# Cos-MLP on float16 pairs, with scales from sums of squares and weight units read and split in two stages

## The chip, the cores and the metric

The kernel runs on one core of a Trainium2 chip. The metric is the device time of one execution in microseconds (us); lower is better. Engines are called by their short names: PE (TensorE), DVE (VectorE), ACT (ScalarE), POOL (GpSimd), SP (the queue that issues the DMAs).

## The reference, cut to what matters

```python
attn = softmax(scale * q @ k.T + decay, causal) @ v      # 4 batches, 8 heads, 576 tokens, 64 wide
x = attn as [2304 tokens, 512]
h = x @ w_in                                             # w_in  [512, 2048] float64
g = h * cos(h)
x = g @ w_out                                            # w_out [2048, 512] float64
P = sinkhorn(softmax(x @ w_gate))                        # 8 experts
out = sum over e of P[:, e] * (relu(x @ w1[e]) @ w2[e])  # w1 [512, 1024], w2 [1024, 512]
```

The two weights of the Cos-MLP come in as 64-bit numbers, and the kernel turns them into 32-bit ones by bit operations.

## The kernel before

There are three stages, one after the other: attention (0 to about 237 us of the span), the Cos-MLP (to 654 us) and the experts (to the end).

**Attention** walks through 16 pairs of heads, seven steps each (112 steps, counted by `x`). In each step the code issues work for PE, then ACT, DVE and POOL, and calls `next(pieces)` every third step (lines 727 to 738). When a pair is done, PE turns its output (`turn_x`, L638), ACT copies it from PSUM to `xf` (`keep_x`, L641) and POOL splits it into a rounded part and a rest (`split_x`, L645 and L646), which go to `XT`.

**The Cos-MLP** holds every operand as a pair: `hi`, the number rounded to the PE type fp32r, and `lo`, the rest. A product is three matmuls (`PASSES`: hi·hi, hi·lo, lo·hi). Tokens are cut into five chunks `CH` of 384, 384, 512, 512 and 512; the 2048 hidden columns into 16 units of 128, in blocks of 3, 4, 5 and 4 units (`BLOCKS`). The 80 items of the main loop are (block, chunk, unit). For item n the code issues `layer1(n)` (12 matmuls, L170), then `layer2(n - 2)` (12 matmuls into four PSUM banks, L831), then `between(n)`:

```python
        nc.scalar.activation(t.bitcast(I32), h, AF.Identity, bias=quarter, scale=INV)      # L187
        nc.vector.scalar_tensor_tensor(t, h, INV, t.bitcast(I32), ALU.mult, ALU.subtract)  # L189
        nc.scalar.activation(t, t, AF.Sin, scale=TWO_PI, bias=shift)                       # L190
        nc.vector.tensor_tensor(h, h, t, ALU.mult)                                         # L193
        nc.scalar.copy(hi, h)                                                              # L194
        nc.vector.tensor_tensor(lo, h, f32(hi), ALU.subtract)                              # L196
```

Inside `between` the code also calls `looking` twice (the survey of the expert weights, an Abs with a sum on ACT over 128 loaded tiles, L781) and `pieces` twice. After the last unit of a block and chunk, `finish` copies (block 0, ACT, L844) or adds (later blocks, DVE, L846) the four banks to `acc`. In the last block it also splits the chunk for the gate logits (`split_x` at line 858: L862 on ACT, L863 and L864 on DVE).

`pieces` prepares the weights. `run_job` works on half a unit (128 x 512): POOL squares the top words (L121), DVE does four operations (L122, L124, L126, L129), POOL rounds and subtracts (L131, L132); each operation of DVE is one call of `next`, the POOL pair another. Six halves (the three units of block 0) are done during attention, the other 26 in the MLP, three calls an item. `W` has eight slots of a unit, so unit u waits until unit u - 8 is done.

**The experts** follow at once: POOL prepares the first weights (`prepare_alone`) and the first group of tokens (`combine_first`, L1147 to L1151) while the MLP ends, and PE then runs float16 matmuls of 128x384 (L1306) and 128x256 (L1427).

All engines work in the order of the code (the schedule is by hand); only the waits are found by the framework. Matrix products without a pair, as `ones` times the column sums (L1270), are plain fp32.

## Time and profile before

| | us |
|---|---|
| median of the three runs | 1992.91 |
| lowest and highest run | 1988.58, 1993.2 |
| the profiled execution | 1989.3 |
| its span, first to last instruction | 1987.6 |
| PE busy | 1951.3 |
| DVE, ACT, POOL busy | 1461.0, 1175.2, 1092.2 |

A busy share is that of the whole span. Matmuls overlap, so the duration of one matmul is longer than the distance to the next; for the pace of PE one reads the distances. The granted clock of PE is given as a part of its full speed.

### The profile page before, as it was taken

The numbers are of one execution on the slowest core, as the hardware profiler recorded it, in microseconds if no ns is written. First come the engines' busy times: TensorE is split into PE (matmuls) and PEld (weight loads), VectorE is DVE, ScalarE is ACT, GpSimd is POOL, SyncE is SP. The second block draws the span as 40 slices with busy tenths as digits, with TensorE's granted clock in tenths as the row PEclk, the third lists the DMA queues.
The fourth block names the chain that finished last, engine by engine and source line by source line (L and its number), as shares of the span: only waits on it lengthen the run. The fifth ranks groups of instructions, "written<-read, shape, count | busy, mean of one in ns | idle before, by whom it ended". The sixth has DMA issues, their size and how long they took to land.

```text
span 1987.6 us, 39931 instructions
## 1 busy us (share of the span) xinstructions
PE 1951.3 (98%) x15056; PEld 1545.1 (78%) x15056; DVE 1461.0 (74%) x3199; ACT 1175.2 (59%) x2449; POOL 1092.2 (55%) x1433
## 2 busy tenths in 40 slices
PE   7999999999999999999999999999999999999998
PEld 6888889898887677777777777777777777777776
DVE  8898677676566577787777777777777777777776
ACT  6888676666544676555565555655555555556543
POOL 7999633121166896554655546545456455565531
PEclk9999999999999999999999999999999999999999
DMA  5454155454311122212022021220212202122022
GB/s 134 102 119 108 49 184 175 134 164 138 101 59 40 49 86 86 63 42 88 28 80 72 31 89 33 78 78 22 88 33 77 78 22 88 33 78 78 12 88 64
DMA packets 143136, 157.58 MB, mean 79 GB/s; under 512 B 64864, under 2 KB 99040, under 8 KB 142944
## 3 DMA queue, kind: packets, MB, share of 16 engines
q1 hardware_dynamic: 142944, 155.04, 26.1%
q8 instruction: 118, 1.93, 0.4%
q14 instruction: 74, 0.61, 0.1%
HBM read 139.71 MB, written 10.37 MB: 76 GB/s over the span
## 4 chain that ended last, share of the span: by engine, by line
PE 90%; DVE 4%; ACT 3%; POOL 2%; issue 1%; DMA 0%; SPq 0%; DVEq 0%; ACTq 0%; POOLq 0%
PE y L1427 19%; PE y L1306 18%; PE bq L1427 14%; PE bq L1306 13%; PE a L831 9%; PE ph L170 8%; PE pv L601 2%; PE pst L551 2%; PE pss L494 1%; PE pss L495 1%; PE pv L581 1%; DVE xt L863 1%; PE psq L375 1%; DVE acc L846 0%; DVE largest L864 0%
## 5 line engine op out<-in xcount | busy, mean ns | idle before, releaser
L1427 PEld LDWEIGHTS <-h 128*128 128x128 f16 x6048 | 590.3, 98 | 77.2 <-POOL h L1341 1.2
L1306 PEld LDWEIGHTS <-wa 128*128 128x128 f16 x4032 | 393.4, 98 | 258.5 <-issue 3.6
L1306 PE MATMUL y<-xc,wa 128*128 128x384 f16 x2304 | 429.8, 326 | 1.9 <-ACT ct L1322 1.0
L1341 POOL TENSOR_TENSOR h<-rt,h 128x384 f16<-128x384 f32 x192 | 175.3, 913 | 448.3 <-ACT h L1340 439.3
L1427 PE MATMUL y<-wb,h 128*128 128x256 f16 x3456 | 408.9, 273 | 0.9 <-POOL h L1341 0.9
L1322 ACT ACTIVATE ct<-y 128x384 f32<-128x384 f32 x192 | 94.4, 491 | 419.3 <-PE y L1306 419.1
L1306 PE MATMUL bq<-xc,wa 128*128 128x384 f16 x1728 | 328.0, 326 | 0.2 <-ACT ct L1322 0.2
L1427 PE MATMUL bq<-wb,h 128*128 128x256 f16 x2592 | 306.7, 273 | 0.2 <-DVE h L1332 0.2
L1408 DVE SCALAR_TENSOR_TENSOR acc<-y,gate,acc 128x256 f32<-128x256 f32 x504 | 212.6, 477 | 48.7 <-PE y L1427 48.7
L831 PE MATMUL a<-H,w 128*128 128x512 f32 (+1 forms) x960 | 213.6, 371 | 4.8 <-ACT H L194 4.3
L170 PE MATMUL ph<-xt,w 128*128 128x512 f32 (+1 forms) x960 | 211.9, 369 | 0.0
L831 PEld LDWEIGHTS a<-H,w 128*128 128x128 f32 x960 | 175.9, 189 | 29.0 <-issue 3.4
L170 PEld LDWEIGHTS ph<-xt,w 128*128 128x128 f32 x960 | 175.5, 188 | 22.7
L1408 DVE SCALAR_TENSOR_TENSOR acc<-bq,gate,acc 128x256 f32<-128x256 f32 x378 | 159.7, 478 | 39.2 <-PE bq L1427 39.1
L1332 DVE TENSOR_TENSOR h<-bq,h 128x384 f16<-128x384 f32 x288 | 158.1, 551 | 3.3 <-ACT h L1329 0.6
L1326 DVE SCALAR_TENSOR_TENSOR bq<-bq,ct 128x384 f32<-128x384 f32 x192 | 107.7, 561 | 65.2 <-PE bq L1306 64.4
L1326 DVE SCALAR_TENSOR_TENSOR bq<-y,ct 128x384 f32<-128x384 f32 x96 | 54.4, 566 | 122.9 <-PE y L1306 118.0
L1329 ACT CAST h<-bq 128x384 f16<-128x384 f32 x288 | 134.6, 483 | 14.2 <-DVE bq L1383 14.0
L131 POOL TENSOR_SCALAR w<-dx 128x512 fp32r<-128x512 f32 x32 | 19.8, 620 | 217.9 <-DVE dx L129 217.9
L1335 POOL TENSOR_TENSOR h<-st,h 128x384 f16<-128x384 f32 x96 | 87.8, 915 | 85.0 <-ACT h L1329 81.0
L1339 ACT ACTIVATE rt<-bq 128x384 f32<-128x384 f32 x192 | 93.8, 488 | 21.8 <-DVE bq L1326 19.2
L1087 POOL TENSOR_TENSOR tm<-sg 128x256 f32<-128x256 f32 x128 | 92.2, 731 | 15.1 <-POOL h L1335 12.3
(234 smaller groups left out, 3175.6 us busy)
## 6 DMA issues: line engine op xcount, KB each, us to landing
xc<-xd SPq DMA_DIRECT2D x105, 384.0 KB
sg<-in_moe_w_dram SPq DMA_DIRECT2D x64, 512.0 KB
seen<-in_moe_w_dram SPq DMA_DIRECT2D x64, 256.0 KB
u<-in_moe_w_dram SPq DMA_DIRECT2D x64, 256.0 KB
stg<-in_moe_w_in_dram SPq DMA_DIRECT2D x16, 512.0 KB
stg<-in_moe_w_out_dram SPq DMA_DIRECT2D x16, 512.0 KB
xd<-xc SPq DMA_DIRECT2D x14, 384.0 KB
q<-q SPq DMA_DIRECT2D x30, 160.0 KB
```

Of the source, the lines that this page charges most:

```text
L170: nc.tensor.matmul(ps[:, 0:n], w[:, ws, kk * P : (kk + 1) * P], XT[j][:, xs, kk, :], start=first, stop=kk == KD - 1 and (ws, xs) == PASSES ...
L831: nc.tensor.matmul(a_of[b, j][x][:, 0:n], w[:, s1, DM + x * P : DM + (x + 1) * P], H[:, s2, 0:n], start=i == 0 and n_ == 0, stop=end and n ...
L1087: return [lambda o=o, x=x, y=y, op=op: nc.gpsimd.tensor_tensor(o, x, y, op) for o, x, y, op in todo]
L1306: nc.tensor.matmul(ps[:, 0:HN], w[:, ws, a, k, :], X[b][:, xs, k, :], start=fresh and n == 0, stop=n == 5, skip_group_check=not fresh,)
L1322: nc.scalar.activation(c, cut(ps), AF.Copy, scale=RAISE)
L1326: nc.vector.scalar_tensor_tensor(cut(c), cut(ps), RAISE, other, ALU.mult, ALU.add)
L1329: nc.scalar.copy(HT[m][c][:, 0, :], src)
L1332: nc.vector.tensor_tensor(HT[m][c][:, 1, :], src, HT[m][c][:, 0, :], ALU.subtract)
L1339: nc.scalar.activation(r, cut(ps), AF.Relu)
L1341: nc.gpsimd.tensor_tensor(HT[m][c][:, 1, :], r, HT[m][c][:, 0, :], ALU.subtract)
L1408: nc.vector.scalar_tensor_tensor(a, v, gate[:, tt, e : e + 1], a, ALU.mult, ALU.add)
L1427: nc.tensor.matmul(ps[:, at_ * HD : (at_ + 1) * HD], HT[m][a][:, s1, c * P : (c + 1) * P], W2T[side][m][:, s2, b, :], start=fresh and m == ...
```

## The change

- `XT`, `W` and `H` become float16 pairs instead of fp32r pairs. The matmuls stay the same in number and shape.
- Float16 needs scales. A chunk of tokens and each half of a weight unit get one power of two each, found from the sum of squares: ACT squares with a sum over the row (`AF.Square`, `accum_out`), one fp32 matmul with `ones` adds over the partitions (`total`), and DVE makes scale and inverse by bit operations (`make_scale`). The inverses are multiplied into the scale operands of `between` and `finish` (`turn_factors`, `block_factors`, `down_factors`), which were constants or absent.
- `run_job` becomes `read_unit` (as before, then the Squares) and `split_unit` (total, scales, ACT multiplies by the scale, POOL rounds and subtracts). In the MLP the splitting of a unit runs beside the reading of the next one.
- `keep_x` writes straight to `acc`; `xf` and the split by pair on POOL are gone. `split_chunk` works on whole chunks: four Squares on ACT, a reduce on DVE, the total, and for each of four parts a multiply, a rounding and a subtraction on POOL. Chunks 0 to 2 are done during attention, chunks 3 and 4 in the first 12 items of the MLP.
- `next(pieces)` comes every second step of attention, `next(splitting)` in the other steps. Nine slots for `W`. One more PSUM bank in the MLP, for the totals. Chunks for the logits have tiles of their own (`XL`, still fp32r). The order of tiles in the experts' memory is another.

```diff
+    def total(cols, c):
+        ps = spare_bank[0]()[:, c : c + cols.shape[1]]
+        nc.tensor.matmul(ps, ones, cols, start=True, stop=True)
+        return ps
+    def make_scale(sums, scale, back):
+        bits = back.bitcast(I32)
+        nc.vector.tensor_scalar(back, sums, 4.0**-LIMIT, 4.0**LIMIT, ALU.max, ALU.min)
         yield
+        nc.vector.tensor_scalar(bits, bits, 0x7F000000, 1, ALU.bitwise_and, ALU.logical_shift_right)
+        nc.vector.tensor_scalar(
+            scale.bitcast(I32), bits, -1.0, float((254 - 64 + TOP) << 23), ALU.mult, ALU.add
+        )
         yield
+        nc.vector.tensor_scalar(bits, bits, 1.0, float((64 - TOP) << 23), ALU.mult, ALU.add)
...
+    def turn_factors(b, j0, j1):
+        for i in range(tiles_of(b)):
+            u = unit(b, i)
+            nc.vector.tensor_scalar(turnv[:, u, j0:j1], bk_x[:, j0:j1], bk_w[:, u, 0:1], INV, ALU.mult, ALU.mult)
...
+    def halves(src, hi, lo):
+        nc.gpsimd.tensor_scalar(hi, src, 1.0, 0.0, ALU.mult, ALU.add)
+        nc.gpsimd.tensor_tensor(lo, src, hi, ALU.subtract)
+    def read_unit(u):
...
+            nc.vector.scalar_tensor_tensor(x, dm, TINY * TINY, x, ALU.is_ge, ALU.mult)
+            yield
+            nc.scalar.activation(
+                w[:, 0, half * DM : (half + 1) * DM], x, AF.Square, accum_out=ws[:, half : half + 1]
+            )
         yield
+    def split_unit(u):
+        tm, ws, w = tmw[u % len(tmw)], wsum[u % 2], W[u % NSLOT]
+        if late_[0]:
+            yield
+            yield
+        ps = total(ws, 0)
+        if late_[0]:
+            yield
+        yield from make_scale(ps, sc_w[:, u], bk_w[:, u])
+        nc.vector.tensor_tensor(both[:, u : u + 1], bk_w[:, u, 0:1], bk_w[:, u, 1:2], ALU.mult)
         yield
+        for half in range(2):
+            c = slice(half * DM, (half + 1) * DM)
+            nc.scalar.activation(tm[:, c], tm[:, c], AF.Copy, scale=sc_w[:, u, half : half + 1])
+            yield
+            halves(tm[:, c], w[:, 0, c], w[:, 1, c])
...
+    def split_chunk(j):
+        c0, n = CH[j]
+        xs = xsum[j % 2]
+        for x in range(KD):
+            nc.scalar.activation(
+                XT[j][:, 0, x, :], acc[:, x, c0 : c0 + n], AF.Square, accum_out=xs[:, x : x + 1]
+            )
+            yield
+        nc.vector.tensor_reduce(xs[:, KD : KD + 1], xs[:, 0:KD], axis=AX.X, op=ALU.add)
+        yield
+        ps = total(xs[:, KD : KD + 1], 2)
+        if late_[0]:
+            yield
+        yield from make_scale(ps, sc_x[:, j : j + 1], bk_x[:, j : j + 1])
+        split_done.add(j)
+        yield
+        for x in range(KD):
+            a = acc[:, x, c0 : c0 + n]
+            nc.gpsimd.tensor_scalar(a, a, sc_x[:, j : j + 1], 0.0, ALU.mult, ALU.add)
+            halves(a, XT[j][:, 0, x, :], XT[j][:, 1, x, :])
+            yield
...
-        nc.scalar.activation(t.bitcast(I32), h, AF.Identity, bias=quarter, scale=INV)
+        nc.scalar.activation(t.bitcast(I32), h, AF.Identity, bias=quarter, scale=sc)
...
-        nc.vector.tensor_tensor(h, h, t, ALU.mult)
+        nc.vector.scalar_tensor_tensor(h, h, up, t, ALU.mult, ALU.mult)
...
             def keep_x(n):
-                nc.scalar.copy(xf, px_of.pop(n)[:, 0:S])
-
-            def split_x(n):
-                for c0, cn, hi, lo in x_parts(n):
-                    nc.gpsimd.tensor_scalar(hi, xf[:, c0 : c0 + cn], 1.0, 0.0, ALU.mult, ALU.add)
-                    nc.gpsimd.tensor_tensor(lo, xf[:, c0 : c0 + cn], f32(hi), ALU.subtract)
+                b, hp = divmod(n, HP)
+                nc.scalar.copy(acc[:, hp, b * S : (b + 1) * S], px_of.pop(n)[:, 0:S])
...
-                if x >= 4 and x % 3 == 0:
+                if x in READY:
+                    splitting = chain(splitting, split_chunk(READY[x]))
+                if x >= 4 and x % 2 == 0:
                     next(pieces, None)
+                if x % 2:
+                    next(splitting, None)
...
                 if b == 0:
-                    nc.scalar.copy(a, ps[:, 0:n])
+                    nc.scalar.activation(a, ps[:, 0:n], AF.Copy, scale=sc)
                 else:
-                    nc.vector.tensor_tensor(a, a, ps[:, 0:n], ALU.add)
+                    nc.vector.scalar_tensor_tensor(a, ps[:, 0:n], sc, a, ALU.mult, ALU.add)
...
+        splitting = chain(split_chunk(3), split_chunk(4))
         for n in range(len(items) + LAG):
+            if n < 12:
+                for _ in range(3 if n < 4 else 2):
+                    next(splitting, None)
...
+            if n < 4:
+                next(pieces, None)
...
-            next(pieces, None)
+            if n < 15 or n % 3:
+                next(pieces, None)
```

## Rows read from the trace of the kernel before

**Rows 1.** The page's part 1: busy time of PE, share of the span, instructions.
```profile
PE 1951.3 (98%) x15056; PEld 1545.1 (78%) x15056; DVE 1461.0 (74%) x3199; ACT 1175.2 (59%) x2449; POOL 1092.2 (55%) x1433
```

**Rows 2.** Busy time by stretch: length, busy us (instructions) by engine, clock, DMA.
```profile
60.00:220.00 160.00, 155.28 (x2184) 142.52 (x2182) 142.22 (x426) 137.02 (x261) 148.40 (x170) 1.00 0.47 105
250.00:273.00 23.00, 23.00 (x117) 21.28 (x116) 17.52 (x28) 18.35 (x45) 9.66 (x10) 0.97 0.62 194
309.00:342.00 33.00, 33.00 (x183) 31.96 (x183) 26.23 (x44) 22.45 (x53) 11.69 (x12) 1.00 0.60 185
566.00:655.00 89.00, 85.10 (x392) 68.68 (x391) 57.12 (x98) 36.45 (x61) 61.48 (x80) 1.00 0.15 50
```

**Rows 3.** Chain that ended last, in order of time: start, us, what.
```profile
323.23 2.08 PE a L831 x12
...
354.45 2.72 PE a L831 x12
...
673.09 1.97 PE y L1427 x18
...
690.01 0.97 PE y L1306 x6
```

**Rows 4.** Groups of PE by shape, 0 to 900 us: busy us, mean ns.
```profile
L831 PE MATMUL a<-H,w 128*128 128x512 f32 x576 | 139.5, 391 | 0.2 <-DVE H L196 0.2
...
L831 PE MATMUL a<-H,w 128*128 128x384 f32 x384 | 74.0, 340 | 4.5 <-ACT H L194 4.3 <-DVE H L196 0.2
```

**Rows 5.** Timeline of PE around one product with ones: start, us, what.
```profile
718.33 0.28 PE L1270 MATMUL bq<-cs,ones 128*128 128x8 f32 x2
718.47 1.13 PE L1306 MATMUL bq<-xc,wa 128*128 128x384 f16 x6
```

**Rows 6.** Groups of ACT by shape, 250 to 550 us.
```profile
L781 ACT ACTIVATE seen<-seen 128x512 f32<-128x512 f32 x61 | 38.4, 630 | 15.6 <-DMA seen<-in_moe_w_dram 15.5
...
L187 ACT ACTIVATE t<-ph,quarter 128x512 int32<-128x512 f32 x36 | 24.9, 692 | 24.8 <-PE ph L170 24.8
...
L844 ACT COPY acc<-a 128x512 f32<-128x512 f32 x12 | 7.1, 588 | 4.7 <-PE a L831 3.9
```

**Rows 7.** Timeline of ACT, 384-wide stretch of block 1.
```profile
327.08 0.62 ACT L781 ACTIVATE u<-u 128x512 f32<-128x512 f32 x1
...
327.81 0.48 ACT L194 CAST H<-ph 128x384 fp32r<-128x384 f32 x1
...
332.70 0.59 ACT L187 ACTIVATE t<-ph,quarter 128x384 int32<-128x384 f32 x1
```

**Rows 8.** Timeline of DVE, end of the item that ACT begins at 332.70 us.
```profile
338.13 0.56 DVE L196 TENSOR_TENSOR H<-ph,H 128x384 fp32r<-128x384 f32 x1 [0.55 <-ACT H L194]
```

**Rows 9.** Groups of DVE by shape, 250 to 550 us.
```profile
L124 DVE SCALAR_TENSOR_TENSOR dx<-stg,dx 128x512 int32<-128x512 int32 x25 | 16.9, 677 | 0.0
...
L799 DVE TENSOR_SCALAR rw<-rw 128x1 int32<-128x1 int32 x1 | 0.2, 153 | 0.0
```

**Rows 10.** Groups of POOL, 0 to 250 us.
```profile
L646 POOL TENSOR_TENSOR xt<-xf,xt 128x384 fp32r<-128x384 f32 (+5 forms) x32 | 25.6, 800 | 2.7
...
L645 POOL TENSOR_SCALAR xt<-xf 128x384 fp32r<-128x384 f32 (+5 forms) x32 | 15.0, 470 | 11.7 <-ACT xf L641 11.7
...
L132 POOL TENSOR_TENSOR w<-dx,w 128x512 fp32r<-128x512 f32 x7 | 9.0, 1287 | 0.6
...
L131 POOL TENSOR_SCALAR w<-dx 128x512 fp32r<-128x512 f32 x7 | 4.3, 619 | 5.4 <-DVE dx L129 5.4
```

**Rows 11.** Timeline where attention meets the MLP: ACT, then PE.
```profile
241.20 0.58 ACT L187 ACTIVATE t<-ph,quarter 128x384 int32<-128x384 f32 x1 [2.73 <-POOL xt L646]
...
246.78 3.97 PE L831 MATMUL a<-H,w 128*128 128x384 f32 x12 [3.10 <-ACT H L194]
```

**Rows 12.** Chain that ended last, in the MLP's last block.
```profile
630.39 2.08 DVE acc L846 x4
...
637.97 1.32 DVE xt L863
```

**Rows 13.** Timeline of POOL: the first group of tokens for the experts.
```profile
616.16 0.51 POOL L1147 TENSOR_SCALAR xc<-acc 128x384 f16<-128x384 f32 x1 [4.78 <-ACT acc L927]
```

**Rows 14.** Groups of ACT: the one table load ahead of the Sin.
```profile
L190 ACT ACT_TABLE_LOAD x1 | 1.3, 1283 | 0.0
```

More of the change, by code (lines that the diff above doesn't have):

```diff
@@ L2 @@
 from contextlib import ExitStack
+from itertools import chain
 from itertools import chain
@@ L74 @@
     const = ctx.enter_context(tc.tile_pool(name="const", bufs=1))
+    first = ctx.enter_context(tc.tile_pool(name="first", bufs=1, side="right"))
     mctx = ExitStack()
@@ L83 @@
     gate = const.tile([P, NT // P, NE], F32, name="gate")
-    XT = [big.tile([P, 2, KD, n], F32R, name=f"xt{j}") for j, (_, n) in enumerate(CH)]
+    acc = first.tile([P, KD, NT], F32, name="acc")
+    stg = [big.tile([P, 2 * DM], F32, name=f"stg{i}") for i in range(2)]
+    tmw = [big.tile([P, 2 * DM], F32, name="tmw0")]
     W = {}
@@ L217 @@
             maskt = ap1.tile([P, S], F32, name="maskt")
[L218 to L219 removed]
+            fr, cur, segm = (tmw[0][:, c : c + w] for c, w in ((0, SL), (SL, SL), (2 * SL, P)))
             cum = ap1.tile([P, 2, SL], F32R, name="cum")
@@ L903, in work @@
         def work():
-            for y in range(NWA2, len(jobs)):
-                while free_at.get(jobs[y][0], 0) > now[0]:
+            second = iter(())
+            for u in range(NWA, NUM):
+                while free_at.get(u, 0) > now[0]:
+                    next(second, None)
                     yield
-                yield from run_job(y, keep)
+                for _ in read_unit(u):
+                    next(second, None)
+                    yield
+                for _ in second:
+                    yield
+                second = split_unit(u)
+            for _ in second:
+                yield
             prep_gate()
```

179 lines of the change are left out of this document (110 added, 69 removed).

## The prediction

> **What bounds the kernel now.** I read the page first: PE is busy 98% of the span [rows 1]. That number says little, since one matmul lasts longer than the distance to the next, so I took the table of stretches next [rows 2]. In the body of the attention (60 to 220 us) PE is busy 155 of 160 us, but POOL 148, DVE 142 and ACT 137: four engines near their limit, PE ahead of them. In the MLP PE is never idle until its last block (566 to 655 us), where it is idle 4 of 89 us. The chain of waits then gives PE's real pace, in groups of 12 matmuls [rows 3]. Fp32r: 2.08 us for 384 columns, 173.3 ns each; 2.72 us for 512, 226.7 ns each. Float16, in the experts: 18 of 256 columns in 1.97 us, 109.4 ns each; 6 of 384 in 0.97 us, 162 ns each. At the granted clock of 1.00 [rows 2], its level of 2.4 GHz, 384 columns are 160 ns and 512 are 213.3 ns. So an fp32r matmul costs 13 ns over its columns and a float16 one 2 to 3 ns. This is where the change can gain.
>
> **PE in the MLP.** Layer 2 has 576 matmuls of 512 columns and 384 of 384 [rows 4]; layer 1 has the same. For 384 columns I take the float16 row: 768 x (173.3 - 162) = 8.6 us. A 512-wide float16 matmul isn't in the trace: at least 213.3 ns (its columns), at most the 226.7 ns of now. I take 215.8, with the 2.5 ns of its float16 neighbours, as shape and type are nearest to them: 1152 x 10.9 = 12.6 us. Together **-21.2 us** (bounds -24 and -8.6). The Trainium skill (TensorE: Matmul & The Clock Gate, Wait — 56 ns, not 53.3 ns?) states 215.7 ns for a 512-wide bf16 matmul at this clock; by it the sum stays as it is.
>
> **The totals.** 16 units and 5 chunks give 21 fp32 matmuls with `ones`. The nearest row, with eight columns, puts the next matmul 0.14 us later [rows 5]: 21 x 0.14 = **+3 us** (bounds 0, if they fall into waits, and 21 x 0.28 = 6). They also wait. PE meets the total of a unit in the code about one item after its last Square, so three groups of 12 later, 5.9 us in a 384-wide stretch at the new pace, while an item's way through ACT and DVE took 6.0 us in a busy one (332.70 to 338.13 + 0.56 = 338.69) [rows 7, 8]. I take **+2 us** (bounds 0 and 15: up to 0.7 us for each).
>
> **ACT and DVE in the MLP.** The trace has no Square; the Abs with a sum is the nearest, 0.63 us, and 0.73 us to the next instruction with the reading of the sum [rows 6, 7]. I take 0.7. The copy by a scale: 0.59 us [rows 6], in a row some 0.5. A unit so adds 2 x 0.7 + 2 x 0.5 = 2.4 us of ACT in the some 3.4 items that its reading takes (nine calls, 2.7 an item), 0.7 us an item. The scale operand of L187 becomes a pointer; L187, which has one already, takes 0.1 us more than the plain copy L844 [rows 6], so another 0.1 us. DVE gets about six small operations a unit at 0.15 us [rows 9], 0.9 us, or 0.3 an item, beside eight of 0.68.
> In the 512-wide stretches this lies beside PE: an item lasts 24 x 215.8 = 5.2 us. In the 384-wide stretch of block 1, ACT was busy 22.5 of 33 us and DVE 26.2 [rows 2]; with eight items there, ACT comes to 28.9 and DVE to about 28.6 of the 31.1 us that PE will need. That is 92%, on queues that hand on to each other, so some waits: +1 us for each of blocks 1 and 2. In block 0 four Squares of chunk 4 and four calls an item come on top: ACT 18.4 [rows 2] + 3 + 5 items x 1 = 26 against some 21 us of PE. Two items of delay are free (H is used two items later), so most of the 5 us is absorbed: +2 us. Together **+4 us** (bounds 0 and 11).
> In the last block PE isn't alone in the chain: DVE's additions, subtractions and maxima stand in it [rows 12]. Of the 8 x 24 x 11.3 + 12 x 24 x 10.9 ns = 5.3 us that PE saves there, I count half as lost: **+2.7 us**. The experts' first tokens on POOL start after ACT's scaling [rows 13], which comes earlier with the MLP; POOL's chain moves along.
>
> **Where the stages meet.** ACT stood 2.7 us for POOL's last split of `xf`, and PE then 3.1 us for `hi` [rows 11]. That split goes. In its place PE meets chunk 3's total, behind four Squares (2.8 us), a reduce and the last `keep_x`: about 4 us of PE, but ahead of work that would have waited anyway. **0 us** (bounds -3 and +3). Block 0's factors are some seven small DVE operations on an idle DVE: nothing.
>
> **Attention.** POOL loses 25.6 + 15.0 = 40.6 us [rows 10] and gets three operations on each of 12 parts: at 512 columns 0.62 + 0.62 + 1.29 us [rows 10], at 384 about 2.0, so 4 x 2.5 + 8 x 2.0 = 26 us. POOL's 148 of 160 becomes some 137. ACT gets 6 Squares and 6 copies for the units and 12 Squares for the chunks: 18 x 0.7 + 6 x 0.5 less some 1 us for the narrow ones = 14.5 us over about 185 us. So 137 of 160 becomes 149.5, 93%. POOL works steps ahead, ACT within the step. I take **+3 us**: a fifth of ACT's work appears, and half of PE's 4.7 idle us [rows 2] doesn't come back (bounds -4, all of that idle, and +14.5, all of ACT's work).
>
> **The sum.** -21.2 + 3 + 2 + 4 + 2.7 + 0 + 3 = -6.5 us, from the profiled execution's 1989.3 to 1982.8 us. That execution lies 3.6 us below the median of the runs, 0.7 above the lowest; from the middle of the three runs' span, 1990.9, the sum gives 1984.4. I say **1984 us**. A measurement of this kernel can tell 0.3%, 6 us, from no change; the forecast is a gain just past that.
>
> **Rivals.**
> *ACT takes over as the bound (slower).* All of ACT's added work in attention falls on the path (14.5 instead of 3), the 24 items of 384 columns in blocks 0 to 2 gain nothing (24 x 24 x 11.3 ns = 6.5 us) and block 0 loses the whole 5 us. 1982.8 + 11.5 + 6.5 + 3 = **2004 us**. For it: the 93%, and that ACT answers PE within a step. Against it: ACT was idle 23 of 160 us [rows 2]. It decides once ACT passes about 95% there and PE's waits name ACT. Chance 0.2.
> *The totals turn into waits (no change).* Each of the 21 stops PE for 0.6 us instead of a tenth: 1982.8 + 10.6 = **1993 us**. For it: 5.9 against 6.0 us above. Against it: in 512-wide stretches there are 7.8 us. Chance 0.18.
> *PE alone counts (faster).* POOL's relief clears PE's idle time in attention, and the queues absorb the rest: 1989.3 - 21.2 + 3 - 3 = **1968 us**. For it: PE was never idle in the MLP's body [rows 2]. Chance 0.2.
> *Square needs another table.* A load of ACT's table takes 1.28 us, and one stood ahead of the first Sin [rows 14]. 52 Squares between Exps or Sins with a load before and after each would be 133 us of ACT, at least 80 on the path: some **2065 us**. Against it: the Abs ran among the Sins all through the MLP with that one load. The Trainium skill (ScalarE activation tables: per-element evaluation and per-set limits, What a function is on this engine) says that two functions in different sets are one load apart and two in one set need none; where Square is, no run here shows. Chance 0.03.
> That the change doesn't do what it says would show as fp32r rows; the types stand in the code.
>
> **How the numbers follow.** Forecast 0.39, ACT 0.2, totals 0.18, PE alone 0.2, table 0.03. The forecast's own range is 1977 to 1991, about three quarters of it past 6 us faster; with PE alone, faster is 0.5. Same: the totals for the most part and a fifth of the forecast, 0.25. Slower: ACT, the table and some of the totals, 0.25. The range reaches from just above PE alone to just under ACT as the bound: 1969 to 2003.
>
> **What would show it.** Right: 12 layer matmuls in 1.95 and 2.59 us in the chain; `ones` rows with gaps under 0.3 us; ACT about 149 of 160 us in attention with a span of it within 3 us of now. Wrong: PE waits that name ACT E or A (attention), ACT Square or the reduce (totals), or DVE's dx; groups of 512 still at 2.7 us; more than four table loads.

## The result, and the profile after

The changed kernel takes 2011.22 us (median of 4 runs, 2009.32 to 2012.78) against 1993.06 us for the kernel before on the same chip: ratio 1.0102, 95% interval 1.0087 to 1.0116. It is slower by 18 us, where 9 us faster was forecast, and outside the range.

PE's steady pace is what the prediction said. The chain that ended last, in the MLP (start, us, what), answers to [rows 3]; the groups of PE by shape answer to [rows 4]:

```profile
404.23 2.61 PE ph L277 x12
406.84 2.59 PE a L940 x12
409.43 2.59 PE ph L277 x12
```
```profile
L940 PE MATMUL a<-H,w 128*128 128x512 f16 x576 | 132.4, 379 | 0.8 <-ACT H L303 0.5 <-DVE H L305 0.3
...
L940 PE MATMUL a<-H,w 128*128 128x384 f16 x384 | 69.6, 330 | 2.0 <-ACT H L303 1.4 <-DVE H L305 0.3
```

Twelve matmuls take 2.59 us for 512 columns, and 1.95 us for 384 (below, 260.07 to 262.02). So the time went elsewhere. Three marks, read from PE's timeline, say where: A, the start of the last pair's turned output; M, the start of layer 2 of the last item; and the end of the span. They stand at 236.70, 650.84 and 1987.6 us before, and at 246.30, 672.11 and 2008.0 after. Attention lost 9.6 us, the MLP 11.7 more, and the experts gave 0.8 back.

The changed kernel runs late, so the same stretch of time holds other work than before. The busy time (columns as in [rows 2]) is therefore shown between marks of the work: first from the turned output of the third pair to that of the fifteenth, before and after; then the first MLP stretch, after.

```profile
64.15:225.25 161.10, 156.37 (x2200) 143.41 (x2199) 141.86 (x426) 136.38 (x260) 148.48 (x170) 1.00 0.46 101
64.83:235.30 170.47, 160.56 (x2210) 145.02 (x2209) 145.80 (x452) 147.96 (x298) 138.58 (x153) 1.00 0.40 93
```
```profile
250.00:273.00 23.00, 19.69 (x106) 11.34 (x107) 19.37 (x40) 18.76 (x48) 13.05 (x14) 0.85 0.48 152
```

The same twelve pairs take 9.4 us longer. ACT is busy 11.6 us more in them and POOL 9.9 us less, close to what was predicted. In the first MLP stretch PE is idle 3.3 of 23 us, where it never was before, and its granted clock is 0.85. PE's waits from 236 to 700 us (in total, times, longest) and its timeline name the places:

```profile
PE totals L130 <- ACT w L183: 8.4, 5, 2.9
PE totals L130 <- DVE xsum L229: 6.3, 1, 6.3
PE totals L130 <- DVE bkw L135: 4.1, 1, 4.1
```
```profile
253.31 0.56 PE L130 MATMUL totals<-xsum,ones 128*128 128x1 f32 x2 [6.30 <-DVE xsum L229]
253.73 4.00 PE L277 MATMUL ph<-xt,w 128*128 128x384 f16 x12
...
260.07 2.11 PE L277 MATMUL ph<-xt,w 128*128 128x384 f16 x12
262.02 2.11 PE L940 MATMUL a<-H,w 128*128 128x384 f16 x12
263.97 0.28 PE L130 MATMUL totals<-wsum,ones 128*128 128x2 f32 x2
264.11 2.11 PE L277 MATMUL ph<-xt,w 128*128 128x384 f16 x12
...
279.46 0.59 PE L130 MATMUL totals<-wsum,ones 128*128 128x2 f32 x2 [2.85 <-ACT w L183]
284.11 0.59 PE L130 MATMUL totals<-xsum,ones 128*128 128x1 f32 x2 [4.06 <-DVE bkw L135]
284.56 5.15 PE L277 MATMUL ph<-xt,w 128*128 128x512 f16 x12
```

A total that finds its sums ready costs 0.14 us (263.97 to 264.11), as [rows 5] said. One that does not stops PE: 18.8 us at seven of the MLP's totals. The group after a long stop then runs at about half speed: 4.00 us in place of 2.11, and 5.15 in place of 2.75 (the duration of an undisturbed 512-wide group, 271.91 us). The granted clock of these stretches is 0.50, its level of 1.2 GHz. The third wait is of another kind: the chunk total at 284.11 waits until DVE has read a unit's total, which lies in other columns of the same PSUM tile.

Not all of the time shows at the totals. Busy time from A to M, before and after (PE's is the first; the rest of a stretch PE stands):

```profile
236.70:650.84 414.14, 405.72 (x1960) 354.92 (x1958) 278.30 (x454) 248.06 (x540) 149.04 (x175) 1.00 0.40 125
246.30:672.11 425.81, 396.93 (x1991) 200.57 (x1989) 302.10 (x566) 291.34 (x636) 169.85 (x193) 0.97 0.40 123
```

PE stands 8.4 us before and 28.9 after. At the lower clock level it is busy for 21.2 us after, 17.8 more than before; half of such time is lost, by the groups above, so the clock costs 8.9 us more (an estimate). With 15 totals of 0.14 us and PE's gain of 21.2 us, that makes 20.5 + 8.9 + 2.1 - 21.2 = 10.3 of the 11.7 us by which the MLP is longer.

### The profile page after: what moved, and what is told of

It is laid out like the page before. It is cut to its first block, busy times and chain, and to the rows that moved or that the text cites. A ratio compares the mean times of both kernels' runs of the same rounds, so it can differ in the third digit from the quotient of the medians.

```text
span 2008.0 us, 40250 instructions
## 1 busy us (share of the span) xinstructions
PE 1946.3 (97%) x15098; PEld 1391.7 (69%) x15098; DVE 1491.6 (74%) x3344; ACT 1228.5 (61%) x2585; POOL 1101.6 (55%) x1429
## 3 DMA queue, kind: packets, MB, share of 16 engines
q8 instruction: 119, 1.95, 0.4%
## 4 chain that ended last, share of the span: by engine, by line
PE 78%; DVE 9%; ACT 6%; POOL 3%; issue 2%; DMA 1%; SPq 0%; DVEq 0%; POOLq 0%; ACTq 0%
PE y L1557 19%; PE y L1436 18%; PE bq L1557 14%; PE bq L1436 13%; PE ph L277 5%; PE a L940 4%; PE pv L708 1%; DVE acc L956 1%; PE pst L658 1%; DVE t L298 1%; ACT t L299 1%; DMA seen<-in_moe_w_dram 1%; DVE ph L302 1%; PE pss L601 1%; PE pss L602 1%
## 5 line engine op out<-in xcount | busy, mean ns | idle before, releaser
L277 PE MATMUL ph<-xt,w 128*128 128x512 f16 (+1 forms) x960 | 208.4, 368 | 1.5 <-POOL xt L163 0.9
L940 PE MATMUL a<-H,w 128*128 128x512 f16 (+1 forms) x960 | 202.0, 359 | 2.8 <-ACT H L303 1.9
L277 PEld LDWEIGHTS <-w 128*128 128x128 f16 x960 | 96.0, 101 | 96.2 <-issue 10.6
L940 PEld LDWEIGHTS <-w 128*128 128x128 f16 x960 | 93.9, 99 | 97.6 <-issue 8.1
L1459 ACT CAST h<-bq 128x384 f16<-128x384 f32 x288 | 134.7, 484 | 14.2 <-DVE bq L1513 14.1
L299 ACT ACTIVATE t<-t,shift 128x512 f32<-128x512 f32 (+1 forms) x80 | 54.3, 678 | 71.2 <-DVE t L298 70.4
```

What stands on the lines that cost most here:

```text
L277: nc.tensor.matmul(ps[:, 0:n], w[:, ws, kk * P : (kk + 1) * P], XT[j][:, xs, kk, :], start=first, stop=kk == KD - 1 and (ws, xs) == PASSES ...
L940: nc.tensor.matmul(a_of[b, j][x][:, 0:n], w[:, s1, DM + x * P : DM + (x + 1) * P], H[:, s2, 0:n], start=i == 0 and n_ == 0, stop=end and n ...
L1459: nc.scalar.copy(HT[m][c][:, 0, :], src)
```

## The experiments

Eighteen kernels ran. The table gives, for one traced execution each, how late A is against the kernel before, by how much the MLP (M - A) and the rest (end - M) are longer than there, and the median time with the ratio to the kernel before on the same chip.

| run | A | MLP | rest | us | ratio, 95% interval |
|---|---|---|---|---|---|
| the change | +9.6 | +11.7 | -0.8 | 2011.2 | 1.0102, 1.0087 to 1.0116 |
| 1 no MLP totals | +9.9 | -0.1 | +4.0 | 2003.5 | 1.0055, 1.0033 to 1.0078 |
| 2 totals later | +9.7 | +20.0 | +2.3 | 2022.0 | 1.0149, 1.0114 to 1.0185 |
| 3 no scales in attention | +5.3 | +10.8 | +4.0 | 2009.1 | 1.0084, 1.0061 to 1.0108 |
| 4 no Squares in attention | +7.4 | +9.4 | +3.8 | 2009.9 | 1.0090, 1.0053 to 1.0127 |
| 5 parts spread | +10.0 | +8.9 | +4.4 | 2014.4 | 1.0117, 1.0089 to 1.0144 |
| 6 survey later | +9.6 | +24.1 | +3.9 | 2028.3 | 1.0187, 1.0160 to 1.0214 |
| 7 chunks together, totals later | +9.7 | +17.5 | +2.3 | 2019.9 | 1.0145, 1.0118 to 1.0171 |
| 8 runs 5, 6, 7 joined | +9.7 | +33.2 | +2.3 | 2039.5 | 1.0248, 1.0225 to 1.0270 |
| 9 no MLP Squares | +9.8 | +1.4 | +4.0 | 2004.2 | 1.0069, 1.0046 to 1.0092 |
| 10 no scales in the MLP | +9.8 | -13.4 | -0.7 | 1990.7 | 1.0005, 0.9994 to 1.0016 |
| 11 run 3 without copies | +5.4 | +10.9 | +2.3 | 2008.1 | 1.0090, 1.0056 to 1.0124 |
| 12 copies on POOL | +14.2 | +7.2 | -0.6 | 2012.4 | 1.0111, 1.0068 to 1.0155 |
| 13 chunk totals changed | +9.9 | +15.2 | +2.3 | 2017.0 | 1.0131, 1.0097 to 1.0166 |
| 14 old pace of pieces | +16.3 | +10.0 | +2.2 | 2016.7 | 1.0130, 1.0093 to 1.0166 |
| 15 no parts in attention | +5.5 | +9.1 | +3.9 | 2008.8 | 1.0090, 1.0054 to 1.0126 |
| 16 edits joined | +10.5 | +11.4 | +2.2 | 2012.7 | 1.0109, 1.0087 to 1.0131 |
| 17 without two of them | +10.5 | +14.2 | -0.3 | 2015.1 | 1.0124, 1.0104 to 1.0145 |
| 18 run 16 with room on POOL | +8.6 | +4.3 | +3.9 | 2006.3 | 1.0084, 1.0065 to 1.0102 |

Where a run leaves the MLP as it is (3 to 5, 11, 14, 15), that column lies between +8.9 and +10.9, against +11.7 for the change itself: differences under 3 us in it say nothing about an edit. The traced execution of run 10 is the fastest of its eight, 5.6 us under their median, so its row flatters it. The column "rest" is explained below. The expectations put PE's stops at totals at 23 us; the rows above add up to 18.8.

**1, no totals in the MLP.**

```diff
     def total(cols, c):
+        if late_[0]:
+            return fixed[:, c : c + cols.shape[1]]
```

> Left out: the 13 unit totals and 2 chunk totals of the MLP (the adding over partitions); the scales there come from fixed columns, the Squares stay. Theory (PE, which works in code order, stands at these totals for ACT's Squares and DVE's reduce, and comes back from each stop at a lower clock): the 23 us of waits at the totals and the half-speed groups after them go, and the time falls by some 24 us, to about 1987; the MLP's end is 11 us later than in the kernel before less 24, so some 3 us earlier than there, while attention keeps its 10 us. Rival (ACT and DVE are overloaded by Squares and copies, and the totals are only where PE shows it): PE then waits for H or ph instead, and the time falls by under 8 us, to 2003 or more. Second rival (the stops cost their 23 us, but the lower clock after them nothing): 1991 to 1996.

The MLP is 11.7 us shorter; the time falls by 7.7, as the rest grows by 4.8. This run shows what stands behind the totals: PE's waits first, then its timeline, then the busy time from A to M.

```profile
PE a L946 <- ACT H L309: 5.2, 5, 1.5
PE a L946 <- ACT acc L960: 2.1, 2, 1.8
```
```profile
309.86 0.58 PE L283 MATMUL ph<-xt,w 128*128 128x512 f16 x1 [1.63 <-POOL xt L168]
311.09 1.01 PE L283 MATMUL ph<-xt,w 128*128 128x512 f16 x2 [0.65 <-POOL xt L169]
311.90 4.70 PE L946 MATMUL a<-H,w 128*128 128x512 f16 x12
```
```profile
246.63:660.72 414.09, 391.45 (x1961) 195.53 (x1959) 301.21 (x566) 291.96 (x636) 170.04 (x193) 0.98 0.41 126
```

With the totals gone, PE is early enough to wait for H, for a finish and for chunk 4's parts on POOL. It still stands 22.6 us from A to M. So 18.8 us of stops are gone and PE stands only 6.2 us less; it is busy 12.1 us at the lower clock level, where it was 21.2. The rival's time came (2003 or more), and the MLP lies between the two forecasts: the stops are real, and behind them ACT and POOL are late too.

**2, totals two items later.**

```diff
-            yield
-            yield
+            for _ in range(5):
+                yield
         ps = total(ws, 0)
```

> Nothing left out: in the MLP each unit total is issued two items after its last Square, where one item lay between, and each chunk total two items after its fourth Square, where none did; scale operations follow in one go. Theory (the stop at a total is a matter of where PE meets it): waits at the totals fall from 23 us to under 4, the clock stays up, the time is 1988 to 1993, within 4 us of the run without totals. Rival (ACT's queue is late by more than two items, as it is overloaded): the waits stay above 12 us and the time above 2000.

No unit total waits for its Squares any more, but the two chunk totals now stop PE for 13.3 us, both for DVE's reduce, and one unit total behind the second stops it for 6.1 us, until DVE has read that chunk's total in the shared tile. The MLP is 8.3 us longer. The run also issues pieces and chunk calls more densely to fit. The theory falls in this form.

**3 and 4, attention without the scales' work, and without the Squares alone.**

```diff
-            nc.scalar.activation(
-                w[:, 0, half * DM : (half + 1) * DM], x, AF.Square, accum_out=ws[:, half : half + 1]
-            )
+            if late_[0]:
+                nc.scalar.activation(
+                    w[:, 0, half * DM : (half + 1) * DM], x, AF.Square, accum_out=ws[:, half : half + 1]
+                )
...
-        ps = total(ws, 0)
-        yield from make_scale(ps, sc_w[:, u], bk_w[:, u])
+        if late_[0]:
+            ps = total(ws, 0)
+            yield from make_scale(ps, sc_w[:, u], bk_w[:, u])
```

> Left out in attention: Squares, totals and the operations that make scales (6 + 12 Squares, 3 + 3 totals, about 40 small DVE operations); scales there are constants. The copies by a scale on ACT, the splitting on POOL and its pace stay. Theory (what was added for the scales makes attention 10 us longer): its last pair comes within 2 us of the kernel before, and the time falls by 8 to 10 us to about 2002. Rival (the pace and the order of the pieces, the whole-chunk splitting on POOL and the one tile that the units now share): the last pair stays 6 to 10 us late, and the time is 2007 to 2011.

> Left out in attention: only the 18 Squares on ACT; totals and scale operations run on constant sums. If ACT's Squares are the cost, the last pair comes within 3 us of the kernel before and the run equals the one without scales; if the small DVE operations and the totals are, it stays 6 to 10 us late; if the shared tile and the pace are, both runs without scales stay late alike.

A comes 4.3 us earlier without all of it and 2.2 us earlier without the Squares: so 2.2 us for 18 Squares, 2.1 for totals and scale operations. The other 5.3 us stay. In the run without scales, PE's idle time names POOL, and POOL's timeline shows why:

```profile
132.02 0.55 PE L724 MATMUL pv<-v,A 128*128 128x64 bf16 x13 [1.37 <-POOL v L491]
...
138.60 0.39 PE L618 MATMUL pss<-k,q 128*128 128x256 f32 x1 [1.10 <-POOL k L529]
```
```profile
128.52 0.92 POOL L166 TENSOR_TENSOR xt<-acc,xt 128x384 f16<-128x384 f32 x1
129.40 0.62 POOL L488 TENSOR_SCALAR v<-vrest 128x512 bf16<-128x512 f32 x1
...
131.34 0.62 POOL L491 TENSOR_SCALAR v<-vrest 128x512 bf16<-128x512 f32 x1
...
135.38 0.93 POOL L166 TENSOR_TENSOR xt<-acc,xt 128x384 f16<-128x384 f32 x1
136.40 0.67 POOL L574 TENSOR_SCALAR k<-k 64x576 fp32r<-64x576 f32 x1
137.15 1.40 POOL L529 TENSOR_TENSOR k<-ktf,k 64x576 fp32r<-64x576 f32 x1
```

Parts of a chunk (L165, L166, L255 in this kernel) stand ahead of the split of V (L491) and the rest of K (L529), and PE starts 0.05 to 0.06 us after each of these ends.

**5, parts every fourth step.**

```diff
             halves(a, XT[j][:, 0, x, :], XT[j][:, 1, x, :])
             yield
+            if not late_[0]:
+                yield
```

> Nothing left out: in attention each part of a chunk (three operations on POOL) is followed by one empty call, so that parts come every fourth step instead of every second. Theory (bursts of chunk parts on POOL hold up attention's own POOL work, the split of V and the rest of K, and PE waits for it): the last pair comes 2 to 5 us earlier than in the changed kernel (9.6 us late there), and POOL is no longer over 92% busy in the stretches 130 to 160 and 190 to 210 us. Rival (what is left without the scales, 5.3 us, comes from the denser pieces of weight units, every second step where it was every third): the last pair stays within 1 us of where it is. The MLP is untouched, so the time should fall by what attention gives, less 4.6 us if a product of the Sinkhorn steps behind the MLP again stands for DVE, as it did in the runs without totals and without scales.

A stays (+10.0). Pair 8 came at +4.7 us in place of +6.6, but pair 10 at +9.0 in place of +8.6: spreading moves the loss.

**6, the survey 12 items later; 7, chunks 3 and 4 together with later totals; 8, both with 5.** Run 6 starts `survey` with 24 empty calls and adds a third Abs in the 512-wide items of blocks 1 and 2. Run 7 issues eight Squares, then both reduces, then both totals, and keeps the later unit totals of run 2. Run 8 also gives attention's totals a PSUM bank of their own.

```diff
+            for _ in range(24):
+                yield
             for n, (x, _) in enumerate(chunks):
...
+            if 23 <= n < 60 and CH[items[n][1]][1] == 512:
+                next(looking[0], None)
...
-        splitting = chain(split_chunk(3), split_chunk(4))
+        splitting = split_chunks(3, 4)
```

> Nothing left out: the survey of the expert weights (two Abs on ACT an item) begins 12 items later and catches up with a third Abs in the 512-wide items of blocks 1 and 2. Theory (in block 0 an item's way through ACT and DVE, one after the other, is longer than PE's part of it, so ACT's queue is what the totals and H wait for): without 1.6 us of Abs in each of the first 12 items the waits at totals in block 0 halve, and the MLP's end comes 8 to 12 us earlier against attention's end. Rival (the totals stand for DVE's reduce and for the shared tile, whatever ACT does): under 4 us.

> Nothing left out: unit totals two items after their Square (as in the first try at this), and chunks 3 and 4 done together: eight Squares, the reduces four calls later, both totals four calls after those, the scales two calls later. Theory (each total needs a distance to its sources of more than the lag of ACT and DVE): waits at totals fall from 23 us to under 5 and the MLP's end comes 7 to 12 us earlier against attention's end, as far as leaving the totals out brought (11.6). Rival (ACT's queue just runs further behind; the time goes to waits for H and for the chunks' parts): under 4 us.

> Nothing left out: the three edits together, and in attention the totals in an idle PSUM bank of their own with one more call between total and scale. By the theory the parts add up: attention ends 4 to 7 us later than in the kernel before instead of 9.6, the MLP gains 10 to 16 us over the kernel before, and the time is 1978 to 1988, below both kernels. Rival (the same engine work, ACT's Squares and copies above all, only shows elsewhere): 1993 to 2005.

All three miss. Without the Abs in its first 12 items, block 0 is 0.8 us shorter (item 15 starts 22.0 us late against 22.8), so ACT's busy time is not what binds there. Items 15 to 60 then take 8.5 us more than in the changed kernel; the Abs that were added are part of that, but ACT also stands 26.5 us there for the loads that they read (2.5 us in the changed kernel). In run 7 the stops at totals fall to 6.1 us, and PE waits for the next things in ACT's and DVE's order:

```profile
PE a L974 <- ACT H L337: 7.3, 7, 2.6
PE a L974 <- ACT acc L988: 5.6, 1, 5.6
PE a L974 <- DVE acc L990: 4.1, 4, 1.5
PE totals L130 <- ACT w L183: 3.5, 2, 2.1
...
PE totals L130 <- DVE bkw L135: 2.6, 1, 2.6
```

**9, no Squares in the MLP; 10, no scales in the MLP.**

```diff
+            if not late_[0]:
+                nc.scalar.activation(
+                    w[:, 0, half * DM : (half + 1) * DM], x, AF.Square, accum_out=ws[:, half : half + 1]
+                )
```

The chunks' Squares are treated in the same way, and in run 10 the totals, `make_scale` and ACT's copies too.

> Left out in the MLP: the 26 + 8 Squares on ACT; totals, scale operations and copies stay and run on old sums. New theory (in blocks 0 to 2 an item's steps on ACT and DVE, in one row, are the bound; a total is only the place where PE meets it): without the Squares the totals find their sums ready and ACT has some 0.8 us less an item; the MLP's end comes at least as much earlier against attention's end as without totals (11.6 us), some 14 us. Rival (the totals and the shared tile themselves): waits at totals for DVE stay, and the gain is the 8 us that PE stood for ACT's Squares.

> Left out in the MLP: Squares, totals, scale operations and ACT's copies by a scale; the pairs are split unscaled. The whole price of the scales in the MLP. Theory (PE's pace came as predicted, and all that was lost is the scales' work): the MLP then gains 16 to 20 us over the kernel before, from attention's end to its own, where the changed kernel loses 11. Rival (the new order of the splitting, with chunks 3 and 4 on POOL at the start of the MLP, costs by itself): it gains under 12, with PE waiting for the chunks' parts on POOL.

Without the Squares the MLP is 10.3 us shorter, between theory and rival, and what still stops PE at totals is DVE, at the two of the chunks:

```profile
PE totals L130 <- DVE bkw L135: 6.4, 1, 6.4
PE totals L130 <- DVE xsum L231: 4.9, 1, 4.9
```

Without all of it the MLP is 25.0 us shorter, 13.4 below the kernel before. Busy time by stretch in that run, columns as in [rows 2]:

```profile
250.00:273.00 23.00, 19.32 (x109) 10.54 (x109) 19.75 (x35) 16.13 (x39) 14.93 (x15) 1.00 0.57 175
246.50:647.29 400.79, 384.02 (x1961) 194.00 (x1959) 291.39 (x491) 257.13 (x542) 173.66 (x193) 1.00 0.42 130
```

PE still idles in the first stretch, but in short gaps, and the clock stays at 1.00. By these two traces the scales cost 25 us in the MLP; by the medians of all runs the two kernels lie 20.5 us apart, 4 us less than by the traces. The 11.7 us that go with the totals and the 10.3 that go with the Squares are not shares of it: a stop at a total that waits for a Square goes with either of the two. No run leaves out both and keeps copies and scale operations, so the price of these two is open. Where 16 to 20 us of gain were expected there, 13.4 came in this trace: from A to M PE still stands 16.8 us, 8.4 more than in the kernel before. By its eight runs (1985 to 1993 us) this kernel is level with the kernel before.

**11, attention without the copies too; 12, the copies on POOL.**

```diff
-            nc.scalar.activation(tm[:, c], tm[:, c], AF.Copy, scale=sc_w[:, u, half : half + 1])
             yield
+            nc.gpsimd.tensor_scalar(tm[:, c], tm[:, c], sc_w[:, u, half : half + 1], 0.0, ALU.mult, ALU.add)
```

> Left out in attention: Squares, totals, scale operations, as before, and ACT's six copies by a scale too. Without scales the last pair was 5.3 us late. If ACT's work is what counts there (4.3 us of copies), it is now 1 to 3 us late; if the pace and the order of the pieces on DVE and POOL do it, it stays 4 to 6 us late.

> Nothing left out: the 32 copies by a scale go from ACT to POOL, in place, ahead of the split. If ACT's row of work is the bound, attention ends 1 to 3 us earlier than in the changed kernel and the MLP gains 3 to 8 us, so 2000 to 2007 us; if POOL's turn is as late as ACT's, or DVE beside POOL is slowed by it, no change within 3 us or a loss.

The cut is that of run 12; run 11 is run 3 with ACT's copy made in the MLP alone. ACT's copies cost attention nothing (+5.4 against +5.3). On POOL the same six copies cost it 4.6 us, while the MLP is 4.4 us shorter, a little more than the 3 us above: POOL has more room there than in attention.

**13, chunk totals on four columns, three calls later; 14, pieces every third step; 15, attention without the chunks' parts.**

```diff
+            for _ in range(3):
+                yield
+            ps = total(xs[:, 0:KD], 2)
...
-                if x >= 4 and x % 2 == 0:
+                if x >= 4 and x % 3 == 0:
...
-            nc.gpsimd.tensor_scalar(a, a, sc_x[:, j : j + 1], 0.0, ALU.mult, ALU.add)
-            halves(a, XT[j][:, 0, x, :], XT[j][:, 1, x, :])
+            if late_[0]:
+                nc.gpsimd.tensor_scalar(a, a, sc_x[:, j : j + 1], 0.0, ALU.mult, ALU.add)
+                halves(a, XT[j][:, 0, x, :], XT[j][:, 1, x, :])
```

> Nothing left out: in the MLP only the two chunk totals change. PE adds the four columns of Squares over the partitions, one call item later (three more calls), and DVE adds the four sums afterwards from PSUM; chunk calls come three an item throughout. Unit totals stay as they are. The runs without totals and without Squares were 11.6 and 10.9 us better in the MLP, the run without both 25. In the one without Squares, PE still stood 4.9 us for the reduce and 6.4 us for the shared tile, both at a chunk total. Theory (these two stops, with the half clock after them, are the larger part of the totals' price): the MLP's end comes 8 to 13 us earlier against attention's end, the time is 1998 to 2003. Rival (ACT and DVE are behind by then, whatever PE meets): PE stands for H or for a finish instead, and it comes under 4 us earlier.

> Nothing left out: in attention the pieces of the weight units come every third step again, as in the kernel before; to fit, the scale operations of a unit are issued in one call, and both copies in one. Copies are not the cost (without them the last pair was 5.4 us late against 5.3). If the denser pieces are the rest, the last pair comes 3 to 5 us earlier than in the changed kernel (9.6 us late there); if the chunks' parts on POOL are, it stays within 1.5 us of that.

> Left out in attention: the parts of chunks 0 to 2 on POOL (12 parts of multiply, rounding and subtraction; the rests are zeroed once at the start, on DVE, which may cost up to 2 us there). Squares, totals, scales stay. If the parts on POOL are what is left of the 9.6 us beside the scales' 4.3, the last pair comes 4 to 6 us earlier; if the pace of the pieces is, under 1.5 us. Spreading the parts brought nothing at the end (10.0), which speaks for the second.

Run 13 could not tell: its first total still stands between the last turned output and layer 1 of item 2, at 253.29 us, since layer 1 of items 0 and 1 is issued ahead, and now waits 6.0 us for the last Square instead of the reduce. That Square is the limit there, not the reduce. In run 14, at the old pace with more work in one call, the pairs come 0.1 us later to 1.7 us earlier than in the changed kernel up to pair 10, and the last one 6.7 us later: the denser pieces are no large part of the loss, though the run changed the packing with the pace. Run 15 shows that the parts on POOL are: A comes 4.1 us earlier, although zeroing the rests on DVE made the first pair 1.5 us later. If they add up, scales 4.3 and parts 4.1 to 5.6 make up the 9.6 us; no run left out both.

**16 to 18, edits joined.** Run 16: a part's three operations in three steps; attention's totals in a bank of their own; six of the eight Squares of chunks 3 and 4 in attention's last pairs; both chunk totals before item 4; unit totals two calls later at the same rate; MLP copies on POOL. Run 17 leaves the last two edits out. Run 18 is run 16 with three parts in two items in the MLP, and the early Squares in the last five steps.

```diff
+    def split_last(*js):
+        for j in js:
+            square_chunk(j, KD - 1)
+            yield
...
+        sums = [total(xsum[j % 3][:, KD : KD + 1], 2 + y) for y, j in enumerate(js)]
...
-        splitting = chain(split_chunk(3), split_chunk(4))
+        splitting = split_last(3, 4)
```

> Nothing left out. Five edits that the runs point to. Attention: the three operations of a chunk's part come in three steps instead of one, a call every step; totals have an idle PSUM bank and a step between total and scale; of chunks 3 and 4 the Squares of the first three quarters move to the last pairs of attention. MLP: both chunk totals come together before item 4, the scales two calls later and the parts then one after the other; unit totals two calls later at the same rate of calls (scale operations in one go); copies by a scale on POOL. By the theory (stops at totals, with the half clock behind them, some 13 us at the two chunk totals and 8 us at the unit totals; POOL's bursts 5.5 us of attention): attention ends 5 to 8 us later than in the kernel before instead of 9.6, the MLP gains 6 to 12 us over the kernel before, and the time is 1983 to 1993. Rival (later totals only pass the stop on to H and the finish, as when they were moved before): the MLP loses again, and the time is 2000 or more.

> Nothing left out: as the run beside it, but unit totals stay one item after their Square and the copies stay on ACT. It tells the two chunk totals from the units: if the chunk totals' two stops are the larger part, the MLP loses 0 to 3 us against the kernel before where the changed kernel loses 11, and the run beside it is another 4 to 10 us better; if they are not, it loses 7 or more.

> Nothing left out: the run with all five edits, but in the MLP a chunk's parts come three in two items instead of three an item, and the early Squares come in the last five steps of attention. In that run no chunk total stopped PE and the MLP was 8 us better than the changed kernel up to item 8; then POOL worked through eight parts without a pause, 20 us, DVE stood 3.7 and 8.1 us for POOL (the squares of the top words, the tile that a unit's second stage reads), and PE for H behind it. Theory (a stage that is moved queues behind other work on the engine it is put on, and the engines that wait for that in order hand it on): with room between the parts DVE's two stops shrink to under 3 us together, items 8 to 13 lose under 5 us instead of 15, the MLP gains 0 to 6 us over the kernel before, attention stays 8 to 10 us late, and the time is 1996 to 2004. Rival (POOL is short of time in all of block 0): the loss moves to layer 1 of items 12 to 14, which then waits for the chunk's parts, and the time stays above 2008.

In run 16 no chunk total stops PE (a unit's total just ahead of them does, 2.5 us), and item 8 starts 14.1 us late where it was 22.6. Then the eight parts stand in a row on POOL, and the loss comes back by another way (DVE's timeline, then PE's):

```profile
285.69 0.69 DVE L181 SCALAR_TENSOR_TENSOR tmw<-dm,tmw 128x512 f32<-128x512 bf16 x1 [3.71 <-POOL dm L173]
...
307.17 0.43 DVE L174 TENSOR_SCALAR tmw<-stg 128x512 int32<-128x512 int32 x1 [8.08 <-POOL w L163]
```
```profile
308.24 4.44 PE L984 MATMUL a<-H,w 128*128 128x512 f16 x11 [5.46 <-DVE H L347]
```

DVE stands 8.1 us for a tile that POOL has still to split, H stands behind that on DVE, and PE stands for H. With room between the parts (run 18) the largest such wait is 5.5 us, and the MLP loses 4.3 us instead of 11.7. It missed its expected 1996 to 2004 by 2 us; items 8 to 13 still lose 8.6 us. By item starts the later unit totals and the copies on POOL together are worth 4.9 us after block 0 (from item 15 to 60, against the kernel before, run 16 gains 4.9 us and run 17 nothing). None of the versions beats the kernel before; run 18 is 4.9 us below the change, with intervals that overlap.

## Why the prediction was wrong

**Right.** PE's pace: 162.5 and 215.8 ns a matmul, -21.2 us. The totals as such: 0.14 us each. The busy sums of ACT and POOL in attention (above). No table load was added (four in all, as before). The last block: from item 60 to 79 the changed kernel gains 3.3 of the 5.3 us, so 2.0 were lost and 2.7 said. POOL's chain into the experts moved along.

**"They also wait ... I take +2 us" (bounds 0 and 15).** This is the step that failed most. Seven totals stopped PE for 18.8 us, and taking all of them out brings 11.7 us. I compared a unit total's distance, 5.9 us, with one item's way through ACT and DVE, 6.0 us, and took a near miss for a small one. What decided was how far ACT and DVE run behind PE: at a total, which PE meets in its order, that lag is shown at once, up to 2.9 us at a unit's and 6.3 at chunk 3's. The 11.7 lie within the bounds; what failed is the choice near their low end, and a range drawn from rivals that each put one term high, when several were high together. I also priced no clock after a stop, though [rows 11] showed it: 12 matmuls of 384 columns in 3.97 us behind a 3.10 us wait. By PE's time from A to M in the changed kernel and in run 1, some 6.2 of the 11.7 us are standing and some 4.5 the clock (half of 21.2 - 12.1 us; an estimate).

**"Where the stages meet: 0 us" (bounds -3 and +3).** Chunk 3's total, foreseen as "about 4 us of PE, but ahead of work that would have waited anyway", waited 6.3 us. Of these, the last `keep_x`, the Squares and the reduce took 3.4 us; ACT came to them late:

```profile
246.22 0.67 ACT L296 ACTIVATE t<-ph,quarter,turnv 128x384 int32<-128x384 f32 x1 [3.48 <-DVE turnv L154]
```

"Block 0's factors" were put at nothing, on an idle DVE. They are short, but stand on DVE behind the last pair's work, and ACT's first step of item 0 now needs them: it stood 3.48 us, and its Sin came 1.9 us after A, where it came 0.5 us before A in the old kernel. Nor were PE's 3.1 us of [rows 11] the split's alone; between the split and `hi`, ACT stood for a load of the survey:

```profile
244.29 0.63 ACT L781 ACTIVATE seen<-seen 128x512 f32<-128x512 f32 x1 [2.50 <-DMA seen<-in_moe_w_dram]
```

Item 1 starts 9.8 us late and item 4 13.6: +3.7 us. Chunk 4's total was priced nowhere but in the 21; it waited 4.1 us for a PSUM tile that it shares with the units.

**"ACT and DVE in the MLP: +4 us" (bounds 0 and 11).** Busy sums against PE's time were the wrong measure. They came out about as predicted: for the eight 384-wide items of block 1 (15 to 22), before and after,

```profile
307.07:341.79 34.72, 34.72 (x194) 33.70 (x192) 27.17 (x45) 23.61 (x55) 13.53 (x14) 1.00 0.62 191
329.86:367.26 37.40, 35.02 (x198) 19.71 (x196) 29.32 (x64) 30.91 (x73) 12.49 (x12) 0.95 0.56 169
```

ACT has 7.3 us more and DVE 2.2, where I had 6.4 and 2.4. No engine but PE is over 83% busy, yet the stretch is 2.7 us longer in place of shorter. And leaving out the Squares alone brings 10.3 us. That fits a row: an item goes through ACT and DVE in turn, three steps on each, and what is put between two of these steps makes the whole row longer. No run tests the row by itself; run 6, with less of ACT's work between the steps in block 0 and only 0.8 us gained, speaks against ACT's part of it alone.

**"Attention: +3 us" (bounds -4 and +14.5).** 9.6 us, inside the bounds. The size was off because I counted the new work on ACT only, and took POOL as relieved. Squares on ACT cost 2.2 us, as a fifth of them would; but totals and scale operations cost 2.1, and the parts on POOL 4.1 or more, on an engine that is 10 us less busy over the same twelve pairs. The old split followed each pair at a fixed step; the new parts come in runs ahead of V and K.

**The rivals.** They were priced as alternatives and came together. "Totals turn into waits" had the mechanism, at 0.6 us each for 21; it was 2.7 us each for seven. "ACT takes over" had the direction, but ACT never came near 95% in attention. The sum by steps after the runs: -21.2 for PE, +25.0 for the scales in the MLP, +2.0 in the last block and +5.9 for the rest there make +11.7; with 9.6 of attention and -0.8 behind the MLP that is +20.5 us in the traced execution. The last 7.9 us are there without scales too: in run 10 PE stands 8.4 us more than before, mostly in waits under 2 us for H and for finishes. What makes ACT and DVE late there, no run measured.

**Open.** Whether the two totals of the chunks or those of the units are the larger part (run 13 missed its aim, and run 17's MLP changed more than one thing): in the changed kernel 10.4 us of the stops are at the chunks' and 8.4 at the units'. How the 25 us divide between Squares, totals, copies and scale operations.

## What to carry to other kernels

An instruction that is put into the order of an engine that is ahead, for the sake of data from engines behind it, shows their lag at once, and the clock may fall behind the stop. Price it by that lag and not by the busy sums; leaving the instruction out can bring less than its stops show, since the engine then meets a part of the lag at its next wait (here 18.8 us of stops, with the clock behind them, and 11.7 us gained without them). Before work is moved to an engine with idle time, look at what stands behind it in that engine's order, and who waits for that. Once a wait is removed, look for the next one in the same order: of nine kernels that moved work in the MLP, five made it 3 us or more longer than the change had. When one kernel runs late, compare stretches by marks of the work and not by the time since the start.

## What the runs showed of the hardware

One small DVE operation took 0.31 us alone, and 0.88 or 4.10 us beside the same work of POOL. It is the third row scaling of the Sinkhorn steps, in the experts, which no edit touched; DVE and PE in run 3, then DVE in the changed kernel:

```profile
760.51 4.10 DVE L1372 TENSOR_TENSOR gate<-gate,rs 128x144 f32<-128x144 f32 x1
...
769.25 0.31 DVE L1372 TENSOR_TENSOR gate<-gate,rs 128x144 f32<-128x144 f32 x1
```
```profile
765.11 0.39 PE L1416 MATMUL bq<-cs,ones 128*128 128x8 f32 x2 [2.67 <-DVE cs L1373]
```
```profile
765.68 0.88 DVE L1356 TENSOR_TENSOR gate<-gate,rs 128x144 f32<-128x144 f32 x1
```

It took 4.07 to 4.10 us in 15 of the 18 traces, and there the rest behind the MLP is 2.2 to 4.4 us longer; in the three others (runs 10, 12, 17), and in both kernels of the study, it took 0.88 to 0.90. In all 20 traces it began 0.08 to 0.11 us before the end of a POOL instruction, and six more followed there without a gap (760.57 to 764.44 in run 3). In the 15 it ended 0.16 to 0.17 us after the last of the six, in the other five as much after the first. What decides between the two, the traces don't show. So 3 to 5 us of an edited kernel's time can belong to this one operation, and the marks inside the trace are the better measure of an edit. The Trainium skill (SBUF — State Buffer, SBUF: two separate sides) says that DVE and GpSimd share a pair of ports as an exclusive lock, held for the whole instruction, against DVE operations with two SBUF inputs among others. The waits agree with it; that DVE can lose the pair to six POOL instructions in a row, or to one, is what these traces add.

The small scale operations show a second case. In the changed kernel each int32 operation on two columns that began while POOL ran an instruction ended 0.02 to 0.03 us after that instruction, 12 in all, so that they took 178 to 1315 ns; the 36 others took 149 to 174 ns. On one column nothing held them: 9 began inside a POOL instruction and took 137 to 153 ns. One of each (DVE, then POOL beside it):

```profile
66.64 1.31 DVE L138 TENSOR_SCALAR scw<-bkw 128x2 int32<-128x2 int32 x1
66.50 1.43 POOL L513 TENSOR_TENSOR k<-ktf,k 64x576 fp32r<-64x576 f32 x1
...
114.03 0.15 DVE L138 TENSOR_SCALAR scx<-bkx 128x1 int32<-128x1 int32 x1
113.34 1.16 POOL L473 TENSOR_TENSOR vrest<-vrest,v 128x512 f32<-128x512 f32 x1
```
